# A fused attention and routed-experts kernel: token rows in token order, a scattered list of row numbers, indirect reads

## The chip, the cores and the metric

The kernel runs on one core of a Trainium2 chip. The metric is device time in microseconds (us), measured from outside the program. The kernel before takes 282.0 us, the median of three runs from 281.85 to 283.14. The core has five engines, each with its own in-order queue of instructions: TensorE (PE; its weight loads are listed as PEld), VectorE (DVE), ScalarE (ACT), GpSimd (POOL) and SyncE (SP). They wait for one another through semaphores. DMAs are issued from SP's queue and from POOL's queue; all of them run on the same 16 DMA engines. Indirect DMAs, which take row numbers from memory, are issued from POOL.

## What is computed

Decayed linear attention for 4 batches of 768 tokens, 8 heads of 64, gives a matrix `x` of 3072 token rows of 512. Then each token goes to one of 8 experts, a two-layer network whose output is scaled by a gate. The reference, cut:

```python
# attention, block by block (64 tokens), per batch b and head h
intra = einsum('bhic,bhjc->bhij', qb, kb) * Dmask          # lam**(i-j), causal
intra = einsum('bhij,bhjd->bhid', intra, vb)
inter = einsum('bhid,bhde->bhie', qb * lam_pow, kv_state)
out[:, :, sl] = intra + inter
kv_state = lam_block * kv_state + einsum('bhsd,bhse->bhde', kb_dec, vb)
# x: rows are tokens, columns head x dim; experts
logits = (x / |x|) @ (expert_emb / |expert_emb|).T / tau
expert_idx = argmax(logits, axis=1)
gate_w = softmax(logits)[expert_idx]
for e in range(E):                                         # E = 8, D = 512, F = 1024
    mask = expert_idx == e
    out[mask] = gate_w[mask, None] * (relu(x[mask] @ w1[e]) @ w2[e])
```

## The kernel before

**Attention stage.** There are 24 token tiles of 128, and the loop `for i in range(-2, R)` makes one step per tile. Its order is written out by hand: what a step issues stands in that order in every engine's queue. In step `i`, PE transposes q and k of tile `i + 2` (`pe_Tq`, L298; `pe_Tk`, L310), turns tile `i - 1`'s finished attention output into token rows (`pe_X`, L394), makes its router scores (`pe_z`, L402; `pe_zT`, L408, one step later), the score matrix of tile `i + 1` (`pe_ST`, L324, masked by DVE into `stm`, L332) and the output of tile `i` (`pe_inter` L345, `pe_O` L355, copied to `xT` by ACT L362 and DVE L363), and updates the state (`pe_kv`, L370). POOL scales k of tile `i + 4` (`pool_ks`, L286). SP issues the loads of k and v some four tiles ahead (L123, L130; three buffers for k, six for v) and of q for two tiles at a time (L116).

**Routing.** Tiles are taken in eight groups: four of four tiles, then four of two. For each group, DVE finds the largest score (`rt_a`) and the one-hot choice (`rt_a2`), POOL takes the square root of the row's norm (`rt_n`, L444), PE counts ranks within each expert (`pe_rank`, L453 to L458), `rt_b` turns rank and expert into a slot number, `rt_c` scales the scores by the norm and ACT exponentiates (L494), `rt_d` makes the gate. Small lists `at(step, slot, ...)` place these inside the steps: `z` is after the scores were evicted and before `pe_z`, `mid` is between the masking of the score matrix and the copies of `xT`, `end` and `pool` close a step.

**Rows to experts.** A token row goes to DRAM as 512 fp16 values, the token's number and its gate (258 words, 1032 bytes), from the buffer `xg`, of which there are three. `scatter` (L503) is an indirect DMA from POOL that writes each of a tile's 128 rows to its slot in `xs_dram`, which has one region of 3072 rows for each of 10 *runs*. Experts 0 and 1 have two runs each, for tiles 0 to 17 (384 slots) and for the rest (128 slots); experts 2 to 7 have one run each (448 slots). Before that, ten `fill` DMAs (L513) write rows with an out-of-range token number into all slots that will be read, so that unused slots are dropped at the end. Expert rows are then plain loads from SP (`load_xe` L522, `load_xh` L527).

**Expert stage.** PE transposes the rows (`xt_copy`, L538), makes the first layer (`pe_L1`, L689, ReLU on ACT L691) and the second (`pe_L2`, L713; half tiles of two experts together, L722). `put` scales by the gate (DVE, L695) and sends the tile to the output by an indirect DMA from POOL (L696), which takes token numbers from the loaded rows. Weights are 32 chunks of 512 KB, four per expert, loaded and cast by POOL DMAs (`load_w`, L268 and L270): 12 during attention, four in the first part of the expert stage, then one behind each of the first 16 puts. Expert 3's buffers come free only when attention's have closed. Expert 0's first run is transposed inside the last attention step (`early_xT`).

A branch for overfull runs stands at the end; it is not taken with this data.

## Time and profile before

| | us |
|---|---|
| median of three runs | 282.0 |
| profiled execution | 280.7 |
| its span, first to last instruction | 278.8 |
| PE busy | 242.3 |
| ACT, DVE, POOL busy | 125.0, 121.2, 114.8 |
| start of the first and of the last `o_ps` matmul of attention (L355) | 18.1, 157.9 |
| end of the last matmuls | 269.4 |

The profiled execution took 280.7 us in all, of which 278.8 are between its first and its last instruction. Data moved by DMA is 53.36 MB, a mean of 191 GB/s; q1 is the queue of SP's DMAs, q0 that of POOL's. The granted clock of TensorE is a share of full speed; over the span it is 0.948. A row of the timeline gives start, duration, engine, line, operation, output and input, and in brackets how long the engine sat idle before it and what ended that. A row of the waits gives total idle time, how many times, and the longest.

### The profile page before, as it was taken

How to read it: one execution, taken by the hardware profiler on the slowest of the kernel's cores; microseconds unless marked ns; L12 is line 12 of the kernel's file. 1: busy time of each engine (PE TensorE's matmuls, PEld its weight loads, DVE VectorE, ACT ScalarE, POOL GpSimd, SP SyncE). 2: the span in 40 equal slices, each digit the busy share in tenths (PEclk: the TensorE clock that was granted, in tenths of full speed). 3: DMA queues.
4: the chain of work that ended last, by engine and by line, in shares of the span. 5: the costliest groups of instructions: out<-in, count | busy, mean ns of one | idle time of the engine just before them, and what ended most of it. 6: DMA issues, size and time to landing. Idle time of an engine off the chain costs nothing.

```text
span 278.8 us, 7320 instructions
## 1 busy us (share of the span) xinstructions
PE 242.3 (87%) x3037; PEld 167.3 (60%) x3037; DVE 121.2 (43%) x335; ACT 125.0 (45%) x285; POOL 114.8 (41%) x145
## 2 busy tenths in 40 slices
PE   5689998899509989978878999999999999999960
...
PEclk9779999999966999999995999999999999999996
DMA  7999999999999999998673114999999999921120
GB/s 164 252 243 215 244 239 228 221 226 208 212 231 242 269 223 254 272 204 158 114 134 116 39 40 83 227 260 230 262 243 258 247 254 256 270 86 75 39 83 34
DMA packets 86714, 53.36 MB, mean 191 GB/s; under 512 B 52358, under 2 KB 80262, under 8 KB 86672
## 3 DMA queue, kind: packets, MB, share of 16 engines
q0 software_dynamic: 16272, 26.25, 44.5%
q1 hardware_dynamic: 70400, 26.56, 41.6%
...
## 4 chain that ended last, share of the span: by engine, by line
PE 70%; DVE 9%; DMA 6%; issue 3%; POOL 3%; SPq 2%; ACT 2%; POOLq 0%; DVEq 0%
PE h_ps L689 16%; PE y_ps L713 16%; PE s_ps L324 9%; PE o_ps L355 6%; PE xps L394 4%; PE k_ps L310 3%; DVE stm L332 3%; PE q_ps L298 3%; PE kaz L402 3%; PE o_ps L345 2%; DMA kn<-in_k_dram 2%; PE kaz L370 2%; DMA xs_dram<-xg,si 2%; PE y_ps L722 2%; DMA qn<-in_q_dram 2%
## 5 line engine op out<-in xcount | busy, mean ns | idle before, releaser
L286 POOL TENSOR_TENSOR ks<-kn,kdec 128x512 f32<-128x512 f32 x24 | 25.1, 1044 | 74.7 <-DMA kn<-in_k_dram 46.4
L689 PE MATMUL h_ps<-xTe,w_sb 128*128 128x448 f16 (+2 forms) x320 | 52.7, 320 | 0.9 <-ACT xTe L679 0.5
L691 ACT ACTIVATE hT<-h_ps 128x448 f16<-128x448 f32 (+2 forms) x80 | 37.6, 480 | 34.4 <-PE h_ps L689 32.7
L713 PE MATMUL y_ps<-w_sb,hT 128*128 128x512 f16 x208 | 47.9, 379 | 0.0
L689 PEld LDWEIGHTS <-w_sb 128*128 128x128 f16 x320 | 28.6, 98 | 23.1 <-issue 1.5
L332 DVE TENSOR_TENSOR stm<-s_ps,step 128x512 f32<-128x512 f32 x48 | 30.9, 685 | 22.8 <-PE s_ps L324 22.7
L695 DVE TENSOR_SCALAR y_sb<-y_ps,x_e 128x512 f32<-128x512 f32 x26 | 19.4, 750 | 45.0 <-PE y_ps L713 45.0
L696 POOL DMA_INDIRECT out_dram<-y_sb,x_e x26 | 26.7, 1027 | 29.4 <-DVE y_sb L695 22.8
L503 POOL DMA_INDIRECT xs_dram<-xg,si x24 | 24.4, 1017 | 24.2 <-DVE z_all L411 15.9
L713 PEld LDWEIGHTS <-hT 128*128 128x128 f16 x208 | 19.6, 98 | 21.5 <-ACT hT L691 0.6
L394 PE MATMUL xps<-ident,xT 128*128 128x128 f32 x96 | 17.0, 292 | 17.1 <-ACT xT L362 11.8
L324 PE MATMUL s_ps<-qT,kT 64*64 64x128 f32 x768 | 28.9, 293 | 2.3 <-DVE qT L300 2.3
L396 ACT ACTIVATE sq<-xps 128x512 f16<-128x512 f32 x24 | 14.3, 596 | 36.7 <-PE xps L394 36.7
L355 PE MATMUL o_ps<-stm,vn 128*64 128x128 f32 x384 | 27.5, 287 | 0.0
L324 PEld LDWEIGHTS s_ps<-qT,kT 64*64 64x64 f32 x768 | 22.7, 143 | 7.6 <-issue 5.1
L355 PEld LDWEIGHTS o_ps<-stm,vn 128*64 128x64 f32 x384 | 21.5, 142 | 4.4 <-issue 3.9
L394 PEld LDWEIGHTS xps<-ident,xT 128*128 128x128 f32 x96 | 11.3, 146 | 19.8 <-ACT xT L362 12.9
L298 PE MATMUL q_ps<-ident,qr 128*128 128x128 f32 x96 | 17.1, 305 | 2.4 <-DVE qr L278 2.4
L540 ACT COPY xTe<-xtr 128x512 f16<-128x512 f16 (+1 forms) x16 | 12.4, 772 | 11.3 <-PE xtr L538 11.3
L300 DVE TENSOR_TENSOR qT<-q_ps,lamq 128x512 f32<-128x512 f32 x24 | 16.3, 680 | 2.2 <-PE q_ps L298 1.3
L312 ACT COPY kT<-k_ps 128x512 f32<-128x512 f32 x24 | 14.3, 596 | 5.9 <-PE k_ps L310 5.9
L270 POOL DMA_DIRECT2D w_sb<-in_moe_w_dram x16 | 12.6, 793 | 9.5 <-DMA w_sb<-in_moe_w_dram 4.8
...
## 6 DMA issues: line engine op xcount, KB each, us to landing
...
out_dram<-y_sb,x_e POOLq DMA_INDIRECT x26, 12.5
```

The costliest lines, as they stand in the source:

```text
L286: nc.gpsimd.tensor_tensor(ks[i], kn[i], kdec[:, i % RB].unsqueeze(2).to_broadcast([P, H, D]), op=ALU.mult)
L298: nc.tensor.transpose(t[:, hp, :], qr[j][:, s, 2 * hp : 2 * hp + 2, :].rearrange("p h d -> p (h d)"), ident)
L324: nc.tensor.matmul(bank["s", h2][ds(64 * m, 64), hp, :], kT[i][ds(64 * h2, 64), hp, ds(64 * m, 64)], q_of(i, hp)[ds(64 * h2, 64)], start=( ...
L332: nc.vector.tensor_tensor(stm[i][:, h2], bank.pop(("s", h2)), step.unsqueeze(1).to_broadcast([P, HP, P]), op=ALU.mult)
L355: nc.tensor.matmul(bank["o", h2][ds(64 * u, 64), b2, :], vn[i][:, 2 * hp + h2, :], stm[i][:, h2, hp, :], start=(i % RB == 0 and b2 == 0), ...
L394: nc.tensor.transpose(xv[:, a], xT_of(t, a), ident)
L503: nc.gpsimd.indirect_dma_start(out=xs_views[groups[gi][j]], out_offset=bass.IndirectOffsetOnAxis(ap=slot_i[gi][:, j : j + 1], axis=0), in_ ...
L689: nc.tensor.matmul(h_ps[:, 0:n], w[:, c, ds(P * fc, P)], xTe[r][:, c, 0:n], start=(c == 0), stop=(c == DC - 1))
L691: nc.scalar.activation(hT[r][:, fc, 0:n], h_ps[:, 0:n], AF.Relu)
L695: nc.vector.tensor_scalar(y, y_ps, x[:, g, DW + 1 : DW + 2].bitcast(FP32), None, op0=ALU.mult)
L696: nc.gpsimd.indirect_dma_start(out=out_views[n_scat[0]], out_offset=bass.IndirectOffsetOnAxis(ap=x[:, g, DW : DW + 1], axis=0), in_=y[:], ...
L713: nc.tensor.matmul(y_ps, hT[r][:, fc, ds(P * g, P)], w[:, fc, :], start=(fc == 0), stop=(fc == FC - 1))
```

## The change

Rows are written in token order. `x_dram` holds 3072 rows of 257 words (the values and the gate); when a group's gate is ready (`rt_d`), SP writes the group's rows with two plain DMAs, one per row parity. What is scattered is a pair of words, the token number twice (`ids`, 8 bytes per token), into `idl_dram`, a list with 512 entries per run; `rt_b` makes the slot number with one more test for ranks past 512 and, in `place`, an exchange of low and high bits, so that a list load finds its entries by partition. One `fill` writes the whole list with pairs (out-of-range number, 0). `load_ids` and `load_idh` read the list into SBUF; `gather` fetches 128 rows of `x_dram` by an indirect DMA from POOL, row numbers from the list's second word; `put` takes token numbers from the first. There are 29 gathers and 29 puts; they share POOL's queue with the weights. Buffers of expert rows are no longer held by puts.

`rt_a` and `rt_a2` move from `mid` to `z`; `rt_c` goes one step later for all but the last group inside the loop, also into `z`, and `rt_d` with it; list scatters start as early as `rt_b` allows. Weights go out in steps 5 to 22 instead of 3 to 19, then one in the first part of the expert stage and one behind each of 19 puts. At the start q is loaded ahead of k and the embedding last, three more warm-up matmuls are made, and `act_q` moves from the middle of a step to its end, that for tile pair 1 one step later. The branch for overfull runs is changed to match; it is left out here.

```diff
...
     DC = DM // P
-    ROWS = N
     DW = DM // 2
-    DM2 = DW + 2
+    DM2 = DW + 1
     tau = float(moe_tau)
...
     CAPS = [CA] * ES + [CB] * ES + [CE] * (E - ES)
+    RW, OV, LW = 4 * P, N, 512
     groups = [[0, 1, 2, 3], [4, 5, 6, 7], [8, 9, 10, 11], [12, 13, 14, 15], [16, 17],
...
     moe_t = ctx.enter_context(tc.tile_pool(name="moe_t", bufs=3))
-    xs_dram = dram.tile([NR * ROWS, DM2], I32, name="xs_dram")
-    xs_views = dram_disjoint_views(xs_dram[:], R)
+    x_dram = dram.tile([N, DM2], I32, name="x_dram")
+    x_rows = x_dram[:].rearrange("(t p s) d -> s p t d", p=64, s=2)
+    idl_dram = dram.tile([P * LW, 2], I32, name="idl_dram")
+    idl_r = idl_dram[:].rearrange("(p t) w -> p t w", p=P)
+    idl_views = dram_disjoint_views(idl_dram[:], R)
     n_out = ES * (GA + 1) + (E - ES) * GE + (E - ES) // 2
...
         nc.sync.dma_start(vn[i], v[b, :, ds(c * P, P), :].rearrange("h p d -> p h d"))
+    load_q(0)
     load_k(0)
-    load_q(0)
     load_k(1)
     load_v(0)
+    load_q(1)
+    load_k(2)
+    load_v(1)
     nc.sync.dma_start(emb_sb, moe_expert_emb)
-    load_k(2)
-    load_q(1)
-    load_v(1)
     idle16 = const.tile([P, 512], FP16, name="idle16")
...
     ebase = [const.tile([P, E], FP32, name=f"ebase{n}") for n in range(2)]
-    tok_iota = const.tile([P, R], I32, name="tok_iota")
+    ovf = [const.tile([P, E], FP32, name=f"ovf{n}") for n in range(2)]
+    ids = const.tile([P, R, 2], I32, name="ids")
+    nobody = const.tile([P, NR * RW // P, 2], I32, name="nobody")
     nsq_all = const.tile([P, R], FP32, name="nsq_all")
     ohcum = [const.tile([P, E], FP16, name=f"ohcum{n}") for n in range(2)]
-    zrow = const.tile([P, DM2], I32, name="zrow")
     en_n = const.tile([E, DC, 2, D], FP32, name="en_n")
     def more_constants():
...
     def last_constants():
-        nc.gpsimd.memset(zrow, 0)
-        nc.gpsimd.memset(zrow[:, DW : DW + 1], OOB_IDX)
+        nc.gpsimd.memset(nobody[:, :, 0], OOB_IDX)
+        nc.gpsimd.memset(nobody[:, :, 1], 0)
         nc.gpsimd.tensor_copy(ident16, ident)
...
                        allow_small_or_imprecise_dtypes=True)
-        for n in range(2):
-            nc.gpsimd.iota(ebase[n], pattern=[[ROWS, E]], base=ES * ROWS, channel_multiplier=0,
+        for t, w, first in ((ebase, RW, 0), (ovf, OV - RW, NR * RW)):
+            for n in range(2):
+                nc.gpsimd.iota(t[n], pattern=[[w, E]], base=ES * w + first, channel_multiplier=0,
+                               allow_small_or_imprecise_dtypes=True)
+            nc.gpsimd.iota(t[0][:, 0:ES], pattern=[[w, ES]], base=first, channel_multiplier=0,
                            allow_small_or_imprecise_dtypes=True)
-        nc.gpsimd.iota(ebase[0][:, 0:ES], pattern=[[ROWS, ES]], base=0, channel_multiplier=0,
-                       allow_small_or_imprecise_dtypes=True)
         for h2 in range(2):
-            nc.gpsimd.iota(tok_iota[ds(64 * h2, 64), :], pattern=[[P, R]], base=h2,
+            nc.gpsimd.iota(ids[ds(64 * h2, 64)], pattern=[[P, R], [0, 2]], base=h2,
                            channel_multiplier=2)
...
     KV = kaz[:, 0 : HP * D].rearrange("p (h d) -> p h d", d=D)
-    for _ in range(11):
+    for _ in range(14):
         nc.tensor.matmul(xps, idle16[:, 0:P], idle16, start=True, stop=True)
...
     def pe_X(t):
...
         if j == 0:
-            nt = len(groups[gi])
             xg[gi] = xgp.tile([P, 4, DM2], I32, name="xg", tag="xg")
-            nc.vector.tensor_copy(xg[gi][:, 0:nt, DW : DW + 1],
-                                  tok_iota[:, groups[gi][0] : groups[gi][0] + nt].unsqueeze(2))
         xv = xps.rearrange("p (u a d) -> p a u d", u=2, a=DC)
...
                              start=False, stop=(j == nt - 2), skip_group_check=True)
+    def place(out_i, v, tmp):
+        nc.vector.tensor_scalar(tmp, v, P - 1, 9, op0=ALU.bitwise_and, op1=ALU.logical_shift_left)
+        nc.vector.tensor_scalar(out_i, v, 7, None, op0=ALU.arith_shift_right)
+        nc.vector.tensor_tensor(out_i, out_i, tmp, op=ALU.bitwise_or)
     def rt_b(gi):
...
         t1 = rsm.tile([P, 4, E], FP32, name="t1", tag="t1")[:, 0:nt]
-        nc.vector.tensor_tensor(t1, pc3, ebase[part_of(gi)].unsqueeze(1).to_broadcast([P, nt, E]),
-                                op=ALU.add)
+        n = part_of(gi)
+        nc.vector.scalar_tensor_tensor(t1, pc3, float(RW), ovf[n].unsqueeze(1).to_broadcast([P, nt, E]),
+                                       op0=ALU.is_ge, op1=ALU.mult)
+        nc.vector.tensor_tensor(t1, pc3, t1, op=ALU.add)
+        nc.vector.tensor_tensor(t1, t1, ebase[n].unsqueeze(1).to_broadcast([P, nt, E]), op=ALU.add)
         nc.vector.tensor_tensor(t1, t1, d["oh"], op=ALU.mult)
-        sf = rsm.tile([P, 4], FP32, name="sf", tag="sf")[:, 0:nt]
-        nc.vector.tensor_reduce(sf, t1, axis=AXL.X, op=ALU.add)
+        vf = rsm.tile([P, 4], FP32, name="vf", tag="vf")[:, 0:nt]
+        nc.vector.tensor_reduce(vf, t1, axis=AXL.X, op=ALU.add)
+        vi = rsm.tile([P, 4], I32, name="vi", tag="vi")[:, 0:nt]
+        nc.vector.tensor_copy(vi, vf)
         si = rsm.tile([P, 4], I32, name="si", tag="si", bufs=4)
-        nc.vector.tensor_copy(si[:, 0:nt], sf)
+        place(si[:, 0:nt], vi, rsm.tile([P, 4], I32, name="vl", tag="vl")[:, 0:nt])
         slot_i[gi] = si
...
         nc.vector.tensor_reduce(es, rt[gi]["pe"], axis=AXL.X, op=ALU.add)
-        nc.vector.reciprocal(xg[gi][:, 0:nt, DW + 1 : DW + 2].bitcast(FP32), es.unsqueeze(2))
+        nc.vector.reciprocal(xg[gi][:, 0:nt, DW : DW + 1].bitcast(FP32), es.unsqueeze(2))
+        t = groups[gi][0]
+        for h2 in range(2):
+            nc.sync.dma_start(x_rows[h2][:, t : t + nt, :], xg[gi][ds(64 * h2, 64), 0:nt, :])
     def scatter(gi, j):
+        t = groups[gi][j]
         nc.gpsimd.indirect_dma_start(
-            out=xs_views[groups[gi][j]],
+            out=idl_views[t],
             out_offset=bass.IndirectOffsetOnAxis(ap=slot_i[gi][:, j : j + 1], axis=0),
-            in_=xg[gi][:, j, :],
+            in_=ids[:, t, :],
             in_offset=None,
         )
-    def fill(r):
-        w = CAPS[r] // 64
-        nc.sync.dma_start(xs_dram[ds(r * ROWS, CAPS[r]), :].rearrange("(p g) d -> p g d", p=64),
-                          zrow[0:64].unsqueeze(1).to_broadcast([64, w, DM2]))
-    xe, xTe, hT = {}, {}, {}
-    def load_xe(r):
-        n = min(CAPS[r] // P, GE)
-        xe[r] = moe_x.tile([P, n, DM2], I32, name="x_e", tag=f"x_e{n}", bufs=4 if n == GE else 2)
-        nc.sync.dma_start(xe[r], xs_dram[ds(r * ROWS, n * P), :].rearrange("(g p) d -> p g d", p=P))
-    def load_xh(e):
-        t = moe_x.tile([P, 1, DM2], I32, name="x_h", tag="x_h", bufs=2)
+    def fill():
+        nc.sync.dma_start(idl_r[:, 0 : NR * RW // P, :], nobody)
+    idl, xe, xTe, hT = {}, {}, {}, {}
+    def load_ids(r0, r1):
+        w = RW // P
+        t = const.tile([P, (r1 - r0) * w, 2], I32, name=f"idl{r0}")
+        nc.sync.dma_start(t, idl_r[:, w * r0 : w * r1, :])
+        for r in range(r0, r1):
+            idl[r] = t[:, w * (r - r0) : w * (r - r0 + 1), :]
+    def load_idh():
+        np_ = (E - ES) // 2
+        t = const.tile([P, np_, 2], I32, name="idh")
+        v = idl_r[:, 0 : NR * RW // P, :].rearrange("p (r g) w -> p r g w", g=RW // P)
         for n in range(2):
-            nc.sync.dma_start(t[ds(64 * n, 64), 0, :],
-                              xs_dram[ds((ES + e + n) * ROWS + GE * P, 64), :])
-        xe["h", e] = t
+            nc.sync.dma_start(t[ds(64 * n, 64)], v[0:64, 2 * ES + n :: 2, GE, :])
+        for n in range(np_):
+            idl["h", ES + 2 * n] = t[:, n : n + 1, :]
+    def gather(r, g):
+        if r not in xe:
+            n = 1 if isinstance(r, tuple) else min(CAPS[r] // P, GE)
+            xe[r] = moe_x.tile([P, n, DM2], I32, name="x_e", tag=f"x_e{n}")
+        nc.gpsimd.indirect_dma_start(
+            out=xe[r][:, g, :], out_offset=None, in_=x_dram[:],
+            in_offset=bass.IndirectOffsetOnAxis(ap=idl[r][:, g, 1:2], axis=0))
     def xt_copy(r, g0, g1, pst):
...
         n = groups[gi][-1] + 2
-        at(n, "mid", rt_a, gi)
-        at(n, "mid", rt_a2, gi)
+        at(n, "z", rt_a, gi)
+        at(n, "z", rt_a2, gi)
         at(n, "pool", rt_n, gi)
...
         at(n + 1, "z", rt_b, gi)
-        at(n + 1, "mid", rt_c, gi)
-        at(n + 1, "end", rt_d, gi)
+        at(n + 1 if gi == GL - 2 else n + 2, "z", rt_c, gi)
+        at(min(n + 2, R - 1), "end", rt_d, gi)
         for j in range(len(groups[gi])):
-            at(min(max(n + 1, 9 + 2 * gi) + (j + 1) // 2, R - 1), "pool", scatter, gi, j)
-    for r in range(NR):
-        at(min(r, 8), "sp", fill, r)
-    for r in range(ES):
-        at(22, "sp", load_xe, r)
-    for i in range(24):
-        if i in (3, 5, 7, 9, 10, 12, 13, 14, 16, 17, 18, 19):
-            at(i, "w", load_w, 1)
+            at(min(n + 1 + (j + 1) // 2, R - 1), "pool", scatter, gi, j)
+    at(0, "sp", fill)
+    at(22, "sp", load_ids, 0, ES)
+    for g in range(GA):
+        at(22, "pool", gather, 0, g)
+    for g in range(GA):
+        at(23, "pool", gather, 1, g)
+    for i in (5, 7, 9, 11, 12, 14, 15, 17, 18, 20, 21, 22):
+        at(i, "w", load_w, 1)
     def early_xT():
...
         run(i, "pe2")
-        if i % 2 == 0:
-            act_q(i // 2 + 2)
         if -1 <= i < R - 1:
...
             state(i)
+        if i % 2 == 0 and i >= 0:
+            act_q(i // 2 + 2)
         pool_ks(i + 4)
-        if i == -2:
+        if i == -1:
+            act_q(1)
             decays(1)
-        if i == -1:
             more_constants()
...
                 nc.scalar.activation(hT[r][:, fc, 0:n], h_ps[:, 0:n], AF.Relu)
-        def put(y_ps, x, g):
+        def put(y_ps, r, g):
             y = moe_y.tile([P, DM], FP32, name="y_sb", tag="y_sb")
-            nc.vector.tensor_scalar(y, y_ps, x[:, g, DW + 1 : DW + 2].bitcast(FP32), None, op0=ALU.mult)
+            nc.vector.tensor_scalar(y, y_ps, xe[r][:, g, DW : DW + 1].bitcast(FP32), None, op0=ALU.mult)
             nc.gpsimd.indirect_dma_start(
                 out=out_views[n_scat[0]],
-                out_offset=bass.IndirectOffsetOnAxis(ap=x[:, g, DW : DW + 1], axis=0),
+                out_offset=bass.IndirectOffsetOnAxis(ap=idl[r][:, g, 0:1], axis=0),
                 in_=y[:],
...
             )
-            if n_scat[0] < 16:
+            if n_scat[0] < 19:
                 load_w(1)
...
                                  start=(fc == 0), stop=(fc == FC - 1))
-            put(y_ps, xe[r], g)
+            put(y_ps, r, g)
         def pe_L2h(e):
...
                                      start=(fc == 0), stop=(fc == FC - 1), skip_group_check=True)
-            put(y_ps, xe["h", e], 0)
+            put(y_ps, ("h", e), 0)
         def counts():
...
             scatter(GL, j)
-        load_w(4)
+        load_w(1)
+        load_ids(ES, NR)
+        load_idh()
         pe_L1(0, range(6, 8))
         pe_xT(1, 0, 2)
-        for r in range(ES, 2 * ES):
-            load_xe(r)
-        load_xe(ES + 2)
-        load_xh(2)
-        load_xe(ES + 3)
         pe_L2(0, 0)
...
         pe_L2(0, 2)
+        for r in range(ES, 2 * ES):
+            gather(r, 0)
+        for g in range(GE):
+            gather(2 * ES, g)
+        gather(("h", ES), 0)
         pe_L1(1)
+        for g in range(GE):
+            gather(2 * ES + 1, g)
         pe_L2(1, 0)
...
             if more:
-                load_xe(r + 2)
-                load_xh(e + 2)
-                load_xe(r + 3)
+                for g in range(GE):
+                    gather(r + 2, g)
             pe_L2(r, 2)
+            if more:
+                gather(("h", e + 2), 0)
             pe_L1(r + 1)
...
             pe_L2h(e)
+            if more:
+                for g in range(GE):
+                    gather(r + 3, g)
             if more:
...

```

## The prediction

> **What bounds the kernel now.** I read the page first: how full TensorE (PE) and the DMA engines are over the span, in 40 slices of 7 us, and what each DMA queue moved.
>
> ```profile
> PE   5689998899509989978878999999999999999960
> ...
> PEclk9779999999966999999995999999999999999996
> DMA  7999999999999999998673114999999999921120
> ...
> q0 software_dynamic: 16272, 26.25, 44.5%
> q1 hardware_dynamic: 70400, 26.56, 41.6%
> ```
>
> Two stages: attention to 158 us (24 steps, one per token tile), experts from there to 271. The DMA engines are full until 132 us and again from 171 to 244; PE is full in the second but has holes in the first. Rates: q1 moved 26.56 MB in 41.6% of 278.8 us = 116 us, 0.229 MB/us; q0 0.212 MB/us. The timeline shows the largest hole:
>
> ```profile
> 71.56 1.09 PE L355 MATMUL o_ps<-stm,vn 128*64 128x128 f32 x16
> ...
> 77.12 1.04 POOL L286 TENSOR_TENSOR ks<-kn,kdec 128x512 f32<-128x512 f32 x1 [10.21 <-DMA kn<-in_k_dram]
> ...
> 79.48 1.05 POOL L444 TENSOR_TENSOR nrm<-nsq_all,half 128x4 f32<-128x4 f32 x1
> ...
> 80.56 0.72 DVE L488 TENSOR_SCALAR nrm<-nrm 128x4 f32<-128x4 f32 x1 [8.03 <-POOL nrm L444]
> ...
> 83.04 1.11 PE L394 MATMUL xps<-ident,xT 128*128 128x128 f32 x4 [9.33 <-ACT xT L362]
> ...
> 88.50 1.42 PE L355 MATMUL o_ps<-stm,vn 128*64 128x128 f32 x16
> ```
>
> A late k tile holds POOL; the norm queued behind it holds DVE in rt_c; the copies of xT queued behind that hold PE. The o_ps matmuls of step 10 start at 71.56, those of step 11 at 88.50: 16.94 us, where an undisturbed step takes 5.02 (steps 1 to 5, 24.21 to 44.27). The waits total it:
>
> ```profile
> POOL ks L286 <- DMA kn<-in_k_dram: 46.4, 9, 10.2
> ...
> PE xps L394 <- ACT xT L362: 11.8, 3, 9.3
> ...
> DVE nrm L488 <- POOL nrm L444: 8.5, 2, 8.0
> ...
> DVE xg L390 <- DMA xs_dram<-xg,si: 3.7, 1, 3.7
> ```
>
> The last row is the second hole, at 144 us: a row buffer not yet free of its scatter; step 22 starts 8.93 us after step 21. Busy time by stage, with clock and DMA share:
>
> ```profile
> core 0: us, PE busy (x) PEld busy (x) DVE busy (x) ACT busy (x) POOL busy (x), PEclk, DMA share, GB/s
> 69.00:132.00 63.00, 49.92 (x923) 41.49 (x923) 36.84 (x103) 26.70 (x67) 33.29 (x34) 0.92 1.08 232
> 144.00:156.00 12.00, 9.57 (x139) 7.83 (x136) 7.33 (x32) 3.97 (x13) 0.23 (x1) 0.72 0.22 69
> 171.00:244.00 73.00, 72.36 (x480) 39.36 (x479) 16.01 (x27) 35.71 (x74) 35.20 (x44) 1.00 1.12 244
> ```
>
> From 69 to 132 PE is busy 49.92 of 63 us while DMA stays full: 13 us lost, DMA first among the causes. In the expert stage PE itself is the bound (72.36 of 73) with DMA full beside it, so nothing is to be won there, and a late transfer would be lost time at once.
>
> **The change, part by part.**
>
> *Fills and scattered rows go.* Ten fills write 3712 rows of 1032 B = 3.83 MB, at q1's rate 16.7 us of all engines. Row scatters were 3.17 MB on q0 (15.0 us), row writes come back as 3.16 MB on SP (13.8 us). Inside the stretch that ends at 132 (four groups of rows written, some 13 scatters of before) this nets 16.7 + 8 - 9 = 16 us. The last k, now landing near 132, could land near 116; an unbroken PE transposes it at 24.21 + 20 x 5.02 - 2.1 = 122.5 (the k transposes start 2.1 ahead of a step's o_ps). DMA no longer leads, if only just. The 11.9 us of the first hole (16.94 - 5.02) goes; what is late next is PE itself.
>
> *The row buffer* is released by an SP write, not by a POOL scatter behind late k tiles, and tok_iota no longer writes into it. Steps 22 and 23 took 8.93 + 4.82; without q and k transposes (0.59 + 0.44) a clean one takes 4.0. Gain 13.75 - 8.0 = 5.7.
>
> *Routing spread out.* rt_a leaves "mid" (between stm and the copy of xT, where 44.27 to 55.84 shows two steps losing 1.5 us) for "z", where DVE idles 1.2 us ahead of each stm; rt_c comes one step later, so a norm may be 5 us later. Steps 7, 10, 14, 18, 19, 20 lost 1.47 + 0.67 + 1.29 + 0.87 + 1.47 + 1.22 = 7.0. rt_b, though, grows from 6 DVE instructions to 11 (one is_ge-mult, one add, three of place; 0.17 to 0.2 us each): 1 us per group, more than the 1.2 us of cover once rt_c stands there too. I keep 2, gain 5.
>
> *SP now waits.* The two row writes of a group wait for rt_d, and SP issues in order: behind them stand k(12), k(16) and k(20). The gate is ready at the start of step 8; then two issues of 0.8 us, k(12) issued near +2.2, landing by the k row's median under load (7.5 us) at +9.7, ks 1.04 later, for a transpose wanted at +11. Bounds: 0 (on time) to 3 us each (10.2, the longest landing, in place of 7.5). I take 2 us for all three, nearer to the median.
>
> *Startup.* q0 ahead of k0, act_q(1) after the first stm, three more warm-up matmuls (0.35 each, done before the first transpose at 7.42). The second step waits at 19.2 for the embedding chain behind k(3) (landing 16.3), whose bytes ahead are unchanged. 0; bounds -2.3 (the PE wait ended at 13.42) to +1. The extra constants are small POOL work under PE's steps.
>
> *Early expert rows.* Before, the load for expert 0 lands 3.0 us after its issue, 6.5 us ahead of its use at 155.7. Now four links follow step 21: row writes (3.0), list load beside them (to about +4.5), three POOL gathers 1.3 apart (scatters: 1.0 and 0.3 idle), landing 2.7 (the least of the scatters). The third lands at 4.5 + 2.6 + 2.7 = +9.8, counted from the start of step 22, and PE has its transposes done at +10.2 where it could have had them at +6.1 (4.0 for step 22, 1.2 and 0.9 in step 23). Cost 4.1; bounds 1 (list early) and 8 (each link by the 4.4 median of the scatters). Queued behind these gathers on POOL: a weight chunk, the last scatters, two norms. The row writes of group 5 must wait until gather 0 has read, gather 1 until they land: about +13, which puts the last norm near +20. rt_c wants it 7.8 us after attention's last matmul (158.1 to 165.9 now), also near +20. The list scatters no longer wait for rt_d, as the row scatters did (11.9 us idle until 155.8), and that pays for the longer chain.
>
> The Trainium skill, DMA: Bandwidth & Descriptors (Rules for kernel authors), speaks against this: transfers under 64 KB are mostly overhead and should be merged. Its fit (Anatomy of one DMA), 2.0 us and bytes over 436 GB/s, would make a link 2.0 to 2.3 us and the wait about 2.5, an estimate. No row here shows an 8-byte scatter; the 132 KB ones land in 2.7 to 3.6 when the queues are quiet.
>
> *Tail.* rt_b's five more instructions stand on the chain oh, rank, rt_c, exp, hT (ACT waits 2.18 us there): +1.0.
>
> *Rows for part 2.* T0 is the first second-layer matmul, 166.9 now. POOL's order is weight, put 0, weight, put 1, weight, put 2, weight, then the gathers (the first at about T0+9.5: 1.04 and 0.8 for each pair, y ready 0.75 after its matmuls). On q0 what is issued first lands first: the put of 173.1 landed at 188.5, behind the chunks issued before it (183.4 to 187.5). From the first chunk's issue at T0+2.8: 6.1 us until it has landed (its quiet row), then three puts at 1.1 and three chunks at 2.1 (256 and 512 KB at the 244 GB/s of the stage) and 0.5 for the gather: T0+19. PE wants it at T0+14 (180.8). Bounds 0 (9.5 + 2.7 = 12.2) and 5; I take 4, since the queue ahead is in the code.
>
> *Rest of the expert stage.* DMA's demand did not grow, and chunks come one per put (19 puts for 16) instead of four at once; the last landed at 243.2, 13 us ahead of use, which covers three puts' delay. Gathers stand behind put and chunk on POOL where SP loads stood free. For experts 4 and 6 PE leaves 7.8 us (one L2 1.73, one L1 6.05) for 4.5 of issue and 2.7 of landing: +1 each. The 29 gathers add 29 x 1.0 us to POOL, busy 35 of 73 us; puts may slip behind six y buffers without cost. A POOL DMA also waits for its eighth predecessor (the chunk of 187.83 went out when that of 171.95 had landed, at 187.54), so a full queue stops POOL as well.
>
> *Clock.* After 1.7 us of idle at 144.4 the clock was 0.5 for 6.8 us; PE's s_ps took 1.99 for 1.10. Waits of 4.1 and 4 may bring that back, 3.4 lost each at most: +2 (0 to 6.8). The Trainium skill, TensorE: Matmul & The Clock Gate (Part 1: The HAM clock gate), has the clock halved after an idle window of about 3.4 us. By the page only the two waits, and no shorter one, could bring it, for about 3.4 lost in all. The row of 1.7 us shows that less is enough here.
>
> **Sum.** Gains 11.9 + 5.7 + 5 = 22.6. Losses 2 + 4.1 + 1 + 4 + 2 + 2 = 15.1. Net -7.5 on the profiled execution's 280.7 (span 278.8 and 1.9 around it) = 273.2; that one lay 1.3 below the median 282.0, so 274.5.
>
> **Rivals.**
> 1. *The list costs nothing* (20%): the gathers land in cover, only rt_b and SP's waits stay. For: DMA idles at 0.1 to 0.2 in the tail. Against: the fixed 2.7 us per link. 282.0 - 22.6 + 3 = 262; with half the early wait 264.
> 2. *SP's wait replaces the fills* (12%): k(12), k(16), k(20) late through the same norm chain: 9 us in place of 2, so 281.5, no change. Against: the norm has a step more.
> 3. *Gathers behind weights* (23%), slower: in 171 to 244 POOL's DMAs land at 12.5 us median, not 2.7. Then gathers for experts 4 and 6 come 4.5 + 12.5 - 7.8 = 9.2 late, the second half as much once the queue drains: 274.5 + 13.8 - 2 = 286, with the clock's other 2 us 288. It decides from a landing above 3.3 us, which a backlog of one chunk makes. Against: weights are spread over 19 puts, three fewer ahead at the start.
>
> **Numbers.** Forecast 45%, its own range 268 to 280. Half a per cent (1.4 us) is what a measurement tells from no change. Faster: 45 + 20 + 3 of rival 2 = 68; same 7; slower 25. 264 to 288 holds the forecast, rival 2, most of rival 1 and half of rival 3.
>
> **What would show it.** k's DMA wait at ks under 20 us, no nrm wait of several us, steps 7 to 21 near 5.0; last o_ps start near 141; early transposes waiting on a gather for 3 to 6 us; a wait at the first part-2 transpose; expert stage else unchanged. Wrong if k stays late after each row write, or if the expert stage's transposes wait on gathers pair by pair.

## The result

The changed kernel takes 308.5 us (median of four runs, 305.3 to 312.2) where the kernel before takes 282.6 beside it: 1.088 times as long, with a 95% interval of 1.077 to 1.099. The prediction was 274.5, range 264 to 288, and 68% for faster. Its sign is wrong, and the time lies above the range. On another chip the ratio was 1.108 (1.096 to 1.120).

The profiled execution took 309.75 us, span 307.9, against 280.7 and 278.8 before. Durations below are from single profiled executions; medians are of all runs, ratios only of those within 1.5% of the fastest of their kernel, and in seven experiments (loop ahead, early rows, old start, spread alone, direct reads, counts' constants, two chunks) the profiled execution lies above that, so there order and waits say more than lengths.

The page of the changed kernel, the rows that answer to those shown of before:

```profile
PE   7569999998996899779369594799959995999950
...
PEclk9977999999999799999959998699977999799995
DMA  7999769199999999989152499699693899482120
...
q0 software_dynamic: 17280, 26.92, 44.5%
q1 hardware_dynamic: 66736, 22.14, 33.5%
```

One slice is 7.7 us. PE's deep hole at 71 to 88 us is gone. New are a DMA digit of 1 inside attention (54 to 62 us), where before the engines were full; a PE digit of 3 at 146 to 154; and a 4 or 5 every few slices in the expert stage, where PE was full before. q1 moved 4.4 MB less.

The timeline answers the two rows that bounded the first hole:

```profile
73.41 1.09 PE L363 MATMUL o_ps<-stm,vn 128*64 128x128 f32 x16
79.55 1.09 PE L363 MATMUL o_ps<-stm,vn 128*64 128x128 f32 x16
...
94.75 1.09 PE L363 MATMUL o_ps<-stm,vn 128*64 128x128 f32 x16
105.57 1.09 PE L363 MATMUL o_ps<-stm,vn 128*64 128x128 f32 x16
```

Step 10 to step 11 takes 6.14 in place of 16.94. But step 14 to step 15 takes 10.82 where it took 5.2. The waits of the changed kernel say what took the place of the old ones:

```profile
POOL ks L294 <- DMA kn<-in_k_dram: 33.0, 9, 7.0
...
PE xtr L568 <- DMA x_e<-x_dram,idl: 11.1, 3, 4.0
...
POOL x_e L557 <- DMA x_dram<-xg: 8.1, 1, 8.1
...
PE k_ps L318 <- POOL ks L294: 7.3, 4, 4.1
...
PE k_xtr L568 <- DMA x_e<-x_dram,idl: 5.1, 2, 4.5
```

The waits on ACT's copy of xT (11.8) and on the norm (8.5) no longer appear among the long ones. PE now waits for k (7.3), and for gathered rows (11.1 and 5.1, and others below them). SP's own waits for the groups' gates (`rt_d`) are below; the prediction put their cost to PE at 2 us for the first three groups, whose share of this row is 22.6:

```profile
SPq L518 <- DVE xg L515: 38.2, 6, 11.2
```

The expert stage by busy time, first the changed kernel, then the kernel before; the columns are the stretch, its length, the busy time of PE, PEld, DVE, ACT and POOL with their instructions, the clock, the DMA share and GB/s:

```profile
159.00:297.00 138.00, 120.68 (x722) 62.75 (x718) 30.28 (x79) 52.92 (x109) 74.60 (x83) 0.92 0.70 151
```
```profile
157.00:270.00 113.00, 110.74 (x722) 59.11 (x718) 28.21 (x67) 53.92 (x111) 50.35 (x59) 1.00 0.78 180
```

The stage is 25 us longer with the same 722 matmul records. PE idles 17.3 us in place of 2.3, and is busy 9.9 us longer for the same work, since the clock is 0.92. Over the stage DMA is less full than before (0.70 for 0.78), but not where rows were late: its share is 1.11 from 177.5 to 187 us and 1.04 from 221 to 229, with weight chunks on the way.

| where (profiled executions) | before | after | difference |
|---|---|---|---|
| `o_ps` of step 1 starts | 24.2 | 27.1 | +2.9 |
| from there to step 22 | 128.0 | 118.9 | -9.1 |
| step 22 to step 23 | 4.8 | 13.1 | +8.3 |
| step 23 to the first layer of run 1 | 15.1 | 19.8 | +4.7 |
| to the first layer of runs 2 and 3 | 10.8 | 17.0 | +6.2 |
| to that of run 4 | 9.2 | 11.5 | +2.2 |
| run 4 to run 5 | 11.9 | 11.9 | 0 |
| run 5 to run 6 | 14.1 | 20.4 | +6.4 |
| run 6 to run 7 | 11.9 | 11.9 | 0 |
| run 7 to run 8 | 14.1 | 19.7 | +5.6 |
| run 8 to the last matmul | 25.3 | 25.3 | 0 |
| last matmul to the end of the span | 9.4 | 11.4 | +2.0 |
| sum | | | +29.1 |

Runs 2 and 3 are the second parts of experts 0 and 1, runs 4 to 9 experts 2 to 7. Most of the loss stands where PE turns to rows not yet used: the first run of expert 0, run 1, part 2, and each second expert after that. The last row of the table lies behind the issue of the last put, and no run here explains it.

### The profile page after: what moved, and what is told of

It is laid out like the page before. It is cut to its first block, busy times and chain, and to the rows that moved or that the text cites. A ratio compares the mean times of both kernels' runs of the same rounds, so it can differ in the third digit from the quotient of the medians.

```text
span 307.9 us, 7392 instructions
## 1 busy us (share of the span) xinstructions
PE 253.9 (82%) x3040; PEld 169.5 (55%) x3040; DVE 127.1 (41%) x367; ACT 126.2 (41%) x285; POOL 144.1 (47%) x177
## 4 chain that ended last, share of the span: by engine, by line
PE 47%; DMA 21%; issue 10%; POOL 8%; DVE 6%; SPq 3%; ACT 0%; POOLq 0%; DVEq 0%
DMA kn<-in_k_dram 10%; PE y_ps L743 9%; PE h_ps L719 8%; DMA x_e<-x_dram,idl 6%; PE s_ps L332 5%; PE o_ps L363 5%; PE y_ps L752 3%; PE k_ps L318 3%; PE xps L399 3%; DMA idh<-idl_dram 3%; PE q_ps L306 2%; PE o_ps L353 2%; PE kaz L378 2%; PE kaz L407 2%; POOL x_e L557 2%
## 5 line engine op out<-in xcount | busy, mean ns | idle before, releaser
L725 DVE TENSOR_SCALAR y_sb<-y_ps,x_e 128x512 f32<-128x512 f32 x29 | 21.8, 751 | 94.4 <-PE y_ps L743 56.0
L719 PE MATMUL h_ps<-xTe,w_sb 128*128 128x448 f16 (+2 forms) x320 | 54.2, 326 | 2.1 <-ACT hT L721 1.6
L743 PE MATMUL y_ps<-w_sb,hT 128*128 128x512 f16 x208 | 50.2, 391 | 1.2 <-ACT hT L721 1.2
L726 POOL DMA_INDIRECT out_dram<-y_sb,idl x26 | 26.4, 1015 | 26.8 <-DVE y_sb L725 21.9
L340 DVE TENSOR_TENSOR stm<-s_ps,step 128x512 f32<-128x512 f32 x48 | 30.8, 682 | 17.2 <-PE s_ps L332 17.1
L557 POOL DMA_INDIRECT x_e<-x_dram,idl x26 | 25.2, 971 | 17.5 <-issue 8.5
L522 POOL DMA_INDIRECT idl_dram<-ids,si x24 | 24.5, 1020 | 13.9 <-DVE dz L428 8.8
L332 PE MATMUL s_ps<-qT,kT 64*64 64x128 f32 x768 | 28.2, 287 | 0.0
L363 PE MATMUL o_ps<-stm,vn 128*64 128x128 f32 x384 | 27.1, 285 | 0.0
L568 PEld LDWEIGHTS <-x_e 128*128 128x128 f16 x104 | 7.8, 109 | 26.4 <-DMA x_e<-x_dram,idl 20.0
L370 ACT COPY xT<-o_ps 128x256 f32<-128x256 f32 x24 | 8.9, 373 | 31.7 <-PE o_ps L363 27.2
L318 PE MATMUL k_ps<-ident,ks 128*128 128x128 f32 x96 | 15.5, 287 | 7.6 <-POOL ks L294 7.3
L568 PE MATMUL xtr<-ident,x_e 128*128 128x128 f16 x92 | 9.3, 241 | 13.3 <-DMA x_e<-x_dram,idl 11.1
L399 PE MATMUL xps<-ident,xT 128*128 128x128 f32 x96 | 16.7, 286 | 2.3 <-DVE xT L371 2.2
```

The source lines that it names most:

```text
L318: nc.tensor.transpose(t[:, hp, :], ks[i][:, 2 * hp : 2 * hp + 2, :].rearrange("p h d -> p (h d)"), ident)
L332: nc.tensor.matmul(bank["s", h2][ds(64 * m, 64), hp, :], kT[i][ds(64 * h2, 64), hp, ds(64 * m, 64)], q_of(i, hp)[ds(64 * h2, 64)], start=( ...
L340: nc.vector.tensor_tensor(stm[i][:, h2], bank.pop(("s", h2)), step.unsqueeze(1).to_broadcast([P, HP, P]), op=ALU.mult)
L363: nc.tensor.matmul(bank["o", h2][ds(64 * u, 64), b2, :], vn[i][:, 2 * hp + h2, :], stm[i][:, h2, hp, :], start=(i % RB == 0 and b2 == 0), ...
L399: nc.tensor.transpose(xv[:, a], xT_of(t, a), ident)
L522: nc.gpsimd.indirect_dma_start(out=idl_views[t], out_offset=bass.IndirectOffsetOnAxis(ap=slot_i[gi][:, j : j + 1], axis=0), in_=ids[:, t, ...
```

## The experiments

The kernel before took 279 to 282 us in every group. A letter stands for each edit of the changed kernel, and later kernels combine them. Edits are cut; `...` marks what is left out.

### A. Row writes three steps later on SP

```diff
+    def rows(gi):
+        nt = len(groups[gi])
         t = groups[gi][0]
         for h2 in range(2):
...
         at(min(n + 2, R - 1), "end", rt_d, gi)
+        at(*((min(n + 5, 22), "sp") if gi < 5 else (R - 1, "end")), rows, gi)
```

Here `n` is a group's last tile plus 2: the two DMAs of `rt_d` move from the end of step `n + 2` to behind the loads of step `n + 5`, for groups 0 to 4.

> The changed kernel, with the row writes of a group issued on SP's queue five steps after the group's last tile and behind that step's k and v loads, no longer right after rt_d; rt_d itself stays. SP runs about three steps ahead of the other engines, so the write finds its data ready. Theory A (SP held by the row writes starves k): in the changed kernel SP waited 38.2 us in six waits at L518 and POOL's ks waited 33.0 us for k; the 22 steps from the start of o_ps of step 1 to that of step 22 took 118.9 us. By A the ks waits fall below 10 us, the steps come near 5.2, those 22 take 109 to 113, and the total falls by 6 to 9. Theory B (k is late because the DMA queues are slow, and SP's wait only stands beside it): ks waits stay above 25 us and the 22 steps within 2 us of 118.9.

300.06 us, ratio 1.076 (1.068 to 1.084). From step 1 to step 22 110.2 us in place of 118.9, every step from 2 to 18 between 4.2 and 5.7. The waits of this kernel:

```profile
PE k_ps L318 <- POOL ks L294: 1.8, 2, 1.0
...
PE k_xtr L571 <- DMA x_e<-x_dram,idl: 9.6, 2, 9.1
```
```profile
POOL ks L294 <- DMA kn<-in_k_dram: 24.2, 6, 6.8
...
POOL idl_dram L525 <- DMA idl<-idl_dram: 9.7, 1, 9.7
```

Theory A: the 8.7 us were SP standing at the row writes with k and v queued behind; 5.8 of them are in step 15 alone (5.06 in place of 10.82). It is not one lucky execution: from step 1 to step 19 it takes 98.2 to 103.5 us in the seven profiled kernels with these writes in their old place, and 91.3 to 96.5 in the nine, F's among them, with them moved. POOL's own wait for k stays at 24.2; my limit of 10 us on that row was wrong, the one that counts is PE's, 7.3 to 1.8. The edit has a price of its own: the three row buffers are held longer, ACT waited 7.9 us at L402 for a row write to land (0.4 us in the changed kernel, for DVE), and steps 19 and 20 took 6.4 and 8.8. And half of the gain was returned at once: PE came to the early transposes sooner and waited 9.6 us there for the gathers (step 22 to 23: 17.6). The ratio's interval therefore still overlaps the changed kernel's 1.077 to 1.099.

### B. The loop's gathers one pair of experts earlier

```diff
+        def ahead(e):
+            for g in range(GE):
+                gather(ES + e, g)
+            gather(("h", e), 0)
+            for g in range(GE):
+                gather(ES + e + 1, g)
...
         pe_xT(3, 0, 1)
+        ahead(ES + 2)
         pe_L1(2)
...
             pe_L2(r, 1)
-            if more:
-                for g in range(GE):
-                    gather(r + 2, g)
             pe_L2(r, 2)
...
             pe_L2(r + 1, 2)
+            if e + 4 < E:
+                ahead(e + 4)
```

The half tile's gather and those of `r + 3` leave their places in the loop in the same way.

> The changed kernel, with the gathers of the expert loop issued one pair of experts earlier on POOL (runs 6 and 7 ahead of run 2's first layer, runs 8 and 9 at the end of the first loop round), so that no put or weight chunk of the current pair stands between them and their use. Theory A (order on POOL): the two transposes' waits of 3.5 and 3.7 us and the half clock after each go; first layer of run 5 to that of run 6 falls from 20.4 to 14.1, run 7 to run 8 from 19.7 to 14.1, the total by about 12. Theory B (the queue behind POOL is full whatever the order): the gathers land in time but weight chunks pushed back behind them come late, first layers wait for w_sb, and the total falls by less than 4.

297.98 median, 292.69 the fastest, beside 279.48. Run 5 to run 6 takes 14.1, run 7 to run 8 14.1: both losses are gone to the tenth, with the chunks and puts all still there. The timeline shows a gather for run 6 and PE's use of it, 22 us apart and with no idle time in brackets:

```profile
203.54 1.00 POOL L557 DMA_INDIRECT x_e<-x_dram,idl  x1 [0.30 <-issue]
...
226.17 0.61 PE L568 MATMUL xtr<-ident,x_e 128*128 128x128 f16 x8
```

In the changed kernel the same gathers go out at 221.05 to 223.64 and PE waits for them from 225.46. Run 4 to run 5 rose from 11.9 to 14.5, a new cost that experiment F explains. For these stretches theory A holds, less 2.6 us.

### C. Early rows: group 4's norm, list and gathers one step earlier

```diff
-        at(n + 1 if gi == GL - 2 else n + 2, "z", rt_c, gi)
...
+        first = gi in (4, GL - 2)
+        at(n + 1 if first else n + 2, "z", rt_c, gi)
...
-    at(22, "sp", load_ids, 0, ES)
+    at(21, "end", load_ids, 0, ES)
```

`rt_d` and the list scatters of group 4 and the gathers of runs 0 and 1 move a step forward likewise.

> The changed kernel, with group 4's norm chain one step earlier (rt_c and rt_d at its n+1), both its list scatters at n+1, and the list load and the gathers of experts 0 and 1 one step earlier, ahead of group 5's row writes. Theory A (the chain row write, list load, gather sets the end of attention, and group 5's row writes stand between the gathers of expert 0 and 1): the list is issued near 141 in place of 145.9, the third gather lands near 151 in place of 157.5, step 22 to 23 falls from 13.1 to 5 to 8, the first layer of run 1 comes 3 to 4.6 sooner after the last attention step, total down 7 to 12. Theory B (the landing times of a backed-up POOL queue set it): the gathers still land 10 us or more after the list is issued, and the total falls by less than 3.

298.22 us, ratio 1.065 (1.057 to 1.073). The list load went out at 141.8 (changed kernel 145.9), as by A, but landed only at 147.8, six microseconds later, beside a weight chunk on POOL's queue that was issued at 139.1 and landed at 147.5. The waits show where POOL stood:

```profile
POOL x_e L557 <- DMA idl<-idl_dram: 8.1, 1, 8.1
```

Step 22 to 23 fell by 1.9 only, to 11.2; the first layer of run 1 came 16.8 after step 23 in place of 19.8, since the gathers for run 1 no longer wait for group 5's row writes. Each theory has half: the order counts, and so does the landing. In the changed kernel one more thing stands between the list, issued at 145.88, and the gathers, a list scatter of group 5:

```profile
149.84 1.02 POOL L522 DMA_INDIRECT idl_dram<-ids,si  x1 [8.63 <-DVE dz L428]
151.17 1.00 POOL L557 DMA_INDIRECT x_e<-x_dram,idl  x1 [0.30 <-issue]
```

It waits until the list has landed: the waits of A name the list load there (9.7 us at L525), and in the seven profiles that record both, the scatter goes out 0.8 us after that landing.

### D. The old start

Loads, copies, tables and warm-up matmuls as before the change.

> The changed kernel with the start as before: k0 ahead of q0, the embedding ahead of k2, eleven warm-up matmuls, q's copy ahead of the first stage's scores, the second decay table two steps before the first output. Theory A (the new start lost 2.9 us): o_ps of step 1 starts near 24.2 in place of 27.1. The total falls by 2.9 if nothing later absorbs it; if SP's row writes set the pace afterwards (k late at steps 7 to 16) it falls by less than 1.5. Theory B (the loss is the longer constant work on POOL, which stays): step 1 still starts near 27 and the total is unchanged.

304.22 us, ratio 1.078 (1.069 to 1.086). Step 1 starts at 24.6. But with the *new* start it also begins at 24.2 to 24.6 in ten of the sixteen profiled executions of this study, and at 26.0 to 27.1 in the other six, the changed kernel's first one among them (24.3 in its second). With the old start it was 24.2 to 24.6 three times in three. The 2.9 us belong to the execution and perhaps to the new start as a risk; they are not a fixed cost of the edit.

### E. Weight chunks behind the part-2 gathers

```diff
-        load_w(1)                       # ahead of load_ids(ES, NR)
...
-            if n_scat[0] < 19:
+            if 3 <= n_scat[0] < 19:
...
             gather(2 * ES + 1, g)
+        load_w(4)
```

> The changed kernel, with the four weight chunks that POOL issues between the last list scatters and the gathers for part 2 (one ahead of the list load, three with run 0's puts) issued together right after those gathers. Theory A (backlog: list load and gathers land 7 us after their issue because the chunks are on their way in the same queue): list and gathers land in 3 to 4, the transposes of run 2 wait less than 1 us in place of 4.0, and from the first layer of run 1 to that of run 2 it is 11 to 12.5 in place of 17.0; the total falls by 4 to 6. Theory B (the list load of 8-byte entries takes 7 to 8 us by itself, and gathers follow it): the list still lands 6 us or more after its issue, and the stretch stays above 15.

Run 1 to run 2 takes 10.8 in place of 17.0, which is what it took before the change. The timeline of this kernel:

```profile
173.45 0.34 SPq L538 DMA_DIRECT2D idl<-idl_dram  x1
173.85 1.25 SPq L548 DMA_DIRECT2D idh<-idl_dram  x2
177.63 1.00 POOL L557 DMA_INDIRECT x_e<-x_dram,idl  x1 [0.30 <-issue]
...
183.77 0.39 PE L568 MATMUL xtr<-ident,x_e 128*128 128x128 f16 x4
```

and of the changed kernel:

```profile
177.50 0.34 SPq L538 DMA_DIRECT2D idl<-idl_dram  x1
177.89 1.64 SPq L548 DMA_DIRECT2D idh<-idl_dram  x2
...
184.45 1.01 POOL L557 DMA_INDIRECT x_e<-x_dram,idl  x1 [2.13 <-issue]
...
191.65 0.61 PE L568 MATMUL xtr<-ident,x_e 128*128 128x128 f16 x4 [3.98 <-DMA x_e<-x_dram,idl]
```

`idh` lands 2.2 us after its issue, not 8.0 (178.83 to 186.80 in the changed kernel's chain), and the gathers in 2.9 to 3.3. So the slow list was not a matter of its 8-byte entries; it was the 512 KB chunks that went out beside it. As a whole this kernel is no faster, 311.61 us, ratio 1.120 (1.103 to 1.137) beside 1.088 and 1.108 of the changed kernel: the four chunks now lay ahead of the loop's first gathers, and PE waited 12.0 us for run 6. The expected fall of 4 to 6 did not come, because the backlog was moved and not removed.

### The fills by themselves

Kernel A, with the ten fills of the kernel before put back at their old steps; they write an area that nothing reads.

> The kernel with the row writes issued later (the first experiment), to which ten zero fills of the size, shape and steps of the kernel before are added; they go to a DRAM area that nothing reads. It prices the fills by themselves, against that first experiment, in which the 22 steps from o_ps of step 1 to step 22 took 110.2 us. Theory A (the fills crowd out k and v): a hole of 8 to 12 us comes back between steps 8 and 12, the 22 steps take 118 to 122, the total rises by 8 to 12. Theory B (the hole of the kernel before came of its routing and its row scatters, not of the fills' bytes): no step is longer than 7, and the 22 steps take less than 113.

317.78 us (314.3 the fastest) against A's 300.06. The 22 steps take 125.7 us in place of 110.2, with steps of 11.5, 8.0, 11.0 and 9.6 among them. Three of its `o_ps` rows:

```profile
72.78 1.09 PE L366 MATMUL o_ps<-stm,vn 128*64 128x128 f32 x16
84.28 1.09 PE L366 MATMUL o_ps<-stm,vn 128*64 128x128 f32 x16
88.43 1.09 PE L366 MATMUL o_ps<-stm,vn 128*64 128x128 f32 x16
```

POOL's waits for k rise from 24.2 to 63.6 us. So the fills are enough to make a hole like that of before: 15.5 us for 3.8 MB, which is also near the 16.7 us of engine time that the prediction worked out for them. What the row scatters added before was not tested.

### The routing spread by itself

The kernel before, with `rt_a` to `z` and, for the first four groups, `rt_c` and `rt_d` a step later (two groups' scatters moved behind them).

> The kernel before, with the routing steps alone spread out: rt_a and rt_a2 behind the copy of z in place of between stm and xT, rt_c and rt_d one step later for the first four groups, row scatters not ahead of rt_d; fills, row scatters and loads as they were. Theory A (prediction's term: steps 7, 14, 18, 19, 20 lose 5.5 us to routing on DVE's path, and spreading returns most of it): the 22 steps take 122 to 125 in place of 128.0, the total falls by 3 to 6. Theory B (those steps lose time to k and v landing late, and DVE's place hides): 127 to 129, total unchanged within 1.5.

281.16 us, ratio 1.003 (0.997 to 1.010): no gain. The profiled execution took 285.5 us, and its 22 steps 132.9, above what either theory has. In it PE's wait for `xT` fell from 11.8 to 4.8, but a wait for ACT's `zT` rose from 1.7 to 8.0. Two more waits of this kernel show what stands ahead of `zT` on ACT, and beside it on DVE:

```profile
PE kaz L370 <- ACT zT L405: 8.0, 3, 3.6
PE xps L394 <- ACT xT L362: 4.8, 2, 2.5
```
```profile
ACT xg L397 <- DMA xs_dram<-xg,si: 12.4, 3, 5.1
```
```profile
DVE xg L390 <- DMA xs_dram<-xg,si: 13.8, 3, 5.6
```

The kernel before has 3.1 and 3.7 in the last two. With `rt_d` a step later row scatters go out later, and the three row buffers come free later: what DVE's order saved was paid there. (POOL's wait for k rose too, from 46.4 to 58.4, and was not separated from it.) So the total is as theory B says, for a reason that neither theory had, and the test does not price the spread in the changed kernel, whose buffers are freed by SP. There, in A, steps 7, 14 and 18 take 5.6, 5.1 and 4.2 where before they took 6.5, 6.3 and 5.9; whether that is the spread or the missing fills was not separated.

### Direct reads

> The changed kernel with each group of gathers replaced by one direct load on SP's queue of as many rows in token order. It leaves out the routing of rows: every expert gets the first rows of x_dram, so its output is not the reference's; the list, its scatters, its loads and the puts stay. Theory A (the losses of the expert stage are the fetch by POOL: its order, its queue and the wait for the list): from the last attention step to the last matmul 112 to 117 us in place of 137.4 (kernel before 112.4), the early transposes wait less than 1 us, the total falls by 25 to 34 to 271 to 280. Theory B (list scatters, list loads and one weight chunk per put cost the time themselves): the stage stays above 125 us.

276.9 us, ratio 0.985 (0.968 to 1.001), with the causes of B, C and E all gone at one stroke. Its stage from the last attention step to the last matmul takes 115.8 us (before 112.4, after 137.4), clock 0.99:

```profile
152.00:268.00 116.00, 112.21 (x718) 59.79 (x718) 29.89 (x79) 53.03 (x110) 49.31 (x57) 0.99 0.85 182
```

Theory A, though the early transposes still waited 2.7 us for their load, against less than 1 by that theory (step 22 to 23: 8.7). List, scatters, list loads, puts through the list and one chunk per put were all there and cost about 3 us in this stage; the other 22 came with the fetch through POOL. How much of them is its order, its queue and its wait for the list, this run alone does not tell.

### F. The causes mended together

A (for groups 0 to 2 only), B, C and E, with the early transposes behind the last attention matmuls and the last three weight chunks of attention behind the gathers of runs 0 and 1.

> The changed kernel with all that the experiments so far point to: row writes of the first three groups five steps later on SP, group 4's norm, list scatters, list load and the gathers of experts 0 and 1 one step earlier, the early transposes behind the last attention matmuls, the last three weight chunks of attention behind the gathers, the four chunks of part 2 behind its gathers, and the expert loop's gathers one pair earlier. If the causes are separate, their gains add: 8.7 (row writes) + 9.4 (loop, net) + 5 to 9 (early rows) + 4 to 6 (part 2) off 304 gives 271 to 277, at or below the kernel before. If they share one cause (what POOL issues moves from one place to another) it stays above 285.

287.37 us, ratio 1.026 (1.011 to 1.041). The last attention step begins at 142.2 (before 157.0, after 159.1), but run 4 to run 5 takes 28.8 us. The total is above 285, where the expectation put one shared cause; the waits of DVE and of PE name another:

```profile
DVE over L781 <- POOL caps L779: 26.4, 1, 26.4
```
```profile
PE y_ps L748 <- DVE y_sb L730: 15.4, 1, 15.4
```

The overflow counts need three small constants from POOL, which wrote them behind seven gathers; DVE stood at the counts with the scaling of rows queued behind. In B the same order cost the 2.6 us. Two ways out: the gathers behind the counts, or the constants earlier.

> The kernel of the four changes taken together, with the gathers of runs 6 and 7 behind the second layers of runs 2 and 3 on POOL in place of ahead of run 2's first layer; nothing else differs. There the overflow counts (POOL's caps and pstart, then DVE) stood behind seven gathers, DVE was idle for 26.4 us up to 200.2, the scaled rows of runs 2 and 3 came after that, and PE waited 15.4 us at L748. Theory A (that wait is POOL's order alone): first layer of run 4 to that of run 5 falls from 28.9 to 11.9, the other stretches stay within 1, and the total is 268 to 274, faster than the kernel before by 2 to 4 per cent. Theory B (puts or weights hold the y buffers): a wait of 8 us or more stays there, and the total stays above 280.

283.72 us, ratio 1.018 (1.007 to 1.028). The 15.4 us wait is gone, but so is B's gain: run 4 to 5 takes 15.8 (2.1 us of waiting for `y_sb`, then half clock), run 5 to 6 20.6, since the gathers for run 6 now go out at 199 to 203, behind nine chunks issued in the 20 us before. Theory A holds for the wait, not for the total.

> The kernel of the four changes taken together, with the overflow counts' constants (pstart, caps) written by POOL at the end of attention, so that DVE's counts do not stand behind the seven gathers for runs 6 and 7; the gathers stay where they were, ahead of run 2's first layer. Theory A (POOL's order alone made the 15.4 us wait): first layer of run 4 to run 5 falls from 28.9 to 12 to 14, runs 6 and 8 keep their 14.0, and the total is 268 to 273, faster than the kernel before by 2 to 4 per cent. Theory B (seven gathers and seven chunks ahead of the puts keep the y buffers taken): a wait above 5 us stays between runs 4 and 5 and the total stays above 277.

> The same kernel with two weight chunks in place of four directly behind the part-2 gathers, and the other two spread over later puts: two chunks fewer ahead of the gathers for runs 6 and 7 and of the puts. If the backlog of chunks still delays gathers or puts in the version with four, this one is 1 to 4 us faster; if not, the two are the same within 1 us; if expert 3's weights become late, its first layer waits for w_sb and it is slower.

289.6 us, ratio 1.026 (1.019 to 1.032), and 288.0, ratio 1.021 (1.015 to 1.027). Run 4 to 5 is 11.9 in both and run 5 to 6 14.1, so theory A is right about the order; the medians with four chunks and with two differ by 1.6 us, less than either spreads. Yet neither is faster: the last attention steps came late (last step at 156.3 and 155.4, with attention code equal to that of 142.2), and ACT and DVE both stood still near 183 to 189 us. From the first of the two:

```profile
DVE y_sb L735 <- remote: 5.8, 1, 5.8
...
ACT xTe L573 <- remote: 5.1, 1, 5.1
...
PE h_ps L729 <- ACT hT L731: 4.7, 1, 4.7
```

> The kernel with the counts ahead of the gathers for runs 6 and 7, and one weight chunk in place of four directly behind the part-2 gathers; the other three follow one per put. That kernel still lost 6.4 us between the first layers of runs 5 and 6 (20.5 for 14.1), with seven chunks issued at 179 to 188 and gathers for run 6 issued at 199 to 203. Theory A (the chunks on their way in POOL's queue make those gathers late): run 5 to run 6 takes 14 to 16, the total falls by 4 to 8 to 276 to 280. Theory B (the gathers are late because POOL issues them behind two puts and a wait for an x buffer): run 5 to run 6 stays above 18 and the total within 2.

> The same, with the counts' constants on POOL written at the start of the kernel, so that DVE's counts wait for nothing on POOL. In the kernel with four chunks PE waited 2.1 us for y_sb between the first layers of runs 4 and 5 and then ran at half clock (15.9 for 11.9). Theory A: that stretch falls to 12 to 13 and the total is 3 to 4 below the kernel with one chunk, 272 to 276, faster than the kernel before by 1 to 3 per cent. Theory B (the late puts, not the counts, hold the y buffers): no change against it.

The first is the kernel with the counts ahead of the gathers, one chunk in place of four behind the part-2 gathers:

```diff
-        load_w(4)
+        load_w(1)
...
-            if 3 <= n_scat[0] < 19:
+            if 3 <= n_scat[0] < 22:
```

289.8 us, ratio 1.019 (1.010 to 1.028), and 290.21, 1.024 (1.018 to 1.031). Run 5 to 6 falls to 14.4 and 14.8 (theory A), run 4 to 5 to 12.3 and 11.9. Again the totals don't follow, and again ACT and DVE stand for 5 to 6 us with "remote" as the releaser, near the first layer of run 2. To tell whether such stops are the edit's, the kernels with four chunks and with one, and the changed kernel, ran once more together on one chip:

> The kernel with the counts ahead of the gathers and four chunks behind the part-2 gathers, once more, beside the one with one chunk and the changed kernel on one chip. It measured 1.0175 of the kernel before on one chip; the kernel with one chunk 1.0188 on another, although its expert stage was 5 us shorter (from run 0's first layer to the last matmul 119.4 for 124.7), because its last attention steps came later and ACT and DVE stood for 5 to 6 us near the first layer of run 2. Theory A (those stops belong to the chip or to the moment, not to the edit): both show them here or neither does, and the one with one chunk is the faster by 3 to 6. Theory B (they come with the edit): this one shows none, that one does, and they stay within 1.5.

> The kernel with one chunk, once more, on the same chip as the one with four. Theory A: 3 to 6 us below it. Theory B: a stop of 5 to 6 us of ACT and DVE between run 1's and run 2's first layers again, and within 1.5 of it.

> The changed kernel itself on this chip, as the base for the sum of the mended causes: 1.0881 of the kernel before was measured. If the mended kernels' gain is theirs and not a chip's, the ratio here is 1.08 to 1.10 and theirs 1.00 to 1.03.

| on one chip | us | ratio to the kernel before |
|---|---|---|
| changed kernel | 311.1 | 1.108 (1.096 to 1.120) |
| mended, four chunks | 287.8 | 1.023 (1.016 to 1.030) |
| mended, one chunk | 277.0 | 0.984 (0.976 to 0.992) |

No row of the three profiles names "remote". Theory A: the stops were not the edit's, and without them the kernel with one chunk is 10.8 us below that with four, more than my 3 to 6. Of the 10.1 us between their profiled executions 7.9 are in the expert stage (run 5 to 6 takes 16.0 for 23.9), and 2.5 are a later start (step 1 at 26.9 for 24.3) that no edit touched. Nor are the stops all that sets the two executions of the one-chunk kernel apart: of 11.2 us, 10.7 lie ahead of the last attention step, where from step 20 to step 23 it took 23.1 us in place of 14.1; why is open. The stage rows of the mended kernel with one chunk, on the chip without the stops:

```profile
51.00:103.00 52.00, 50.96 (x996) 43.02 (x995) 38.70 (x112) 27.22 (x69) 26.99 (x28) 1.00 1.02 197
```
```profile
142.00:264.00 122.00, 112.01 (x718) 58.60 (x714) 30.11 (x79) 54.47 (x111) 78.94 (x89) 1.00 0.88 184
```

In the middle of attention PE is busy 50.96 of 52 us at full clock, and the last attention step starts at 141.1, 15.9 sooner than before the change: the gain that the prediction saw. That it meets its "near 141" is partly luck, since this kernel has the row writes and the early transposes in other places than the one predicted. The expert stage still takes 122.4 us to the last matmul, 10.0 more than before; PE idles 10.0 of 122, and its clock is 1.00. ACT still waits 4.7 us for a row buffer, in steps 18 to 20. So this version beats both kernels by a little on that chip, while on the chip with the stops it was 1.9% slower than the kernel before. I don't call it faster in general.

## Why the prediction was wrong, step by step

The step that failed is the price of the indirect reads. The forecast let every link land as on a quiet queue (2.7 us for a gather) and held the losses apart; in the changed kernel PE could use a pair of gathers only 6.5 us after the second was issued, behind puts and chunks, and from step 22 to the last matmul 33.4 us were lost where the terms for these parts come to 13.1 (4.1, 1, 4, 2 and 2 for the clock). Replacing the gathers by plain loads took 21.7 us out of the stage behind attention. The second step is SP's wait, 8.7 for 2. Term by term:

- **Fills and scattered rows go** (11.9 us gained): right. The first hole shrank by 10.8, and the fills alone are worth 15.5.
- **The row buffer** (5.7): 4.8 of it. Step 22 takes 4.1 in place of 8.9. The rest, in step 23, was lost to the early rows.
- **Routing spread out** (5): not there by itself (ratio 1.003), since a later `rt_d` holds the row buffers; that price of the move was not in my list. Inside the changed kernel a part of it may be real (steps 7, 14 and 18 of A), which stays open.
- **SP now waits** (2, bounds 0 to 9 for three groups): the mechanism right, the size wrong; 8.7 by experiment A. I took the median of a k load's landing and a gate ready at the start of step 8. But SP runs two to three steps ahead of the other engines (it stood at the first row write from 48.7 us, PE's step 5, to 59.4, in step 7), so a wait for a step's gate takes away all of that lead, for v and q as well as for k. Rival 2 had 9 us for it, by another path (the norm chain).
- **Startup** (0, bounds to +1): 2.9 lost in the first profile, none in ten other executions with the same start.
- **Early expert rows** (4.1, bounds 1 to 8): 8.3. The chain is the one forecast, its links longer. Counted from PE's first matmul of step 22 (143.46), the third gather was to land at +9.8 and landed at +14.0. The list landed near 149.1 (an estimate: the scatter of group 5 at 149.84, less the 0.8), 1.1 later than reckoned; then came the 0.8, 1.3 for that scatter, which the sum does not have, and 1.0 because the last gather landed after 3.7 in place of 2.7: 4.2 together. What was not seen at all: one step of the delay is the change's own, as `rt_c` of group 4 stands one step later and the list load stands behind its row writes (experiment C).
- **Tail** (+1): 4.7 to the first layer of run 1. I had the wait of run 1's gathers for group 5's row writes, and took it as covered; POOL stood there 8.1 us, and PE waited 1.7 at run 1's transposes and 1.7 more for ACT. The rest is in part half clock, up to 163.0.
- **Rows for part 2** (4, bounds 0 to 5): 6.2, and 2.2 more up to run 4. The mechanism, gathers behind chunks and puts, is as told, and experiment E removes the 6.2 in full. I left the list loads, which are on SP, out of the backlog: `idh` took 8.0.
- **Rest of the expert stage** (+1 at experts 4 and 6): 6.4 and 5.6. I took 2.7 for a landing; in the changed kernel PE went on 6.5 after the second gather's issue and 7.8 after the first's. Waits there are 3.5 and 3.7, the rest is the clock.
- **Clock** (2, at most 6.8): six stretches at 0.5 up to the last matmul, 37.6 us long together, where the kernel before had four of 23.9. PE was busy 9.9 us longer in the expert stage alone.

The sum promised 7.5 us. For steps 1 to 22 it had 19.8 (11.9 for the hole, 4.9 for step 22, 5 for the spread, less 2 for SP), and 9.1 came; everywhere else it allowed 12.3 of loss, and 38.2 came. Rival 3 named the right mechanism at 23% and priced the loop at 13.8 (12.0 measured), and its point of decision, a landing above 3.3 us, was passed (6.5). It still ended at 288, because it kept the other terms at the forecast's values: a backlog that delays the loop's gathers delays the list and the part-2 gathers too, and each delay that reaches PE also costs clock. These were largely one case, not five independent sizes, and that case should have carried the main forecast, since the queue ahead stood in the code.

The Trainium skill, TensorE: Matmul & The Clock Gate (Part 1: The HAM clock gate), says that an idle window of about 3.4 us halves the clock and that the window is free-running. Here the waits of 4.1, 4.5, 4.0, 3.5 and 3.7 us each came with a stretch at 0.5, begun within the wait or at most 0.5 us after it, of 3.4, 10.2, 6.8, 6.8 and 3.4 us, multiples of that window; the 1.6 us wait at 155.9 lies inside one. But an idle time as long as the window is not needed. The start's stretch followed one of 2.8 us, and the 6.8 us at 0.5 of the kernel before one of 1.7, while the 2.9 us that PE waited at L306, up to 14.05, came with none. In the 3.4 us ahead of the changed kernel's six stretches PE was busy for 0.1 to 1.0 us, and for 1.5 ahead of that one in the kernel before. So a window in which PE is busy for less than half was enough in these cases, with no single wait of its length.
